# Products of states and w_in for two slices at once, x loads moved, spare matmuls in the prologue

## The chip, the core and the metric

The kernel runs on one core of a Trainium2 chip. The core has a matrix engine (TensorE, "PE" in the profile, with its weight loads as "PEld"), a vector engine (DVE), a scalar engine (ACT), a general engine (POOL) and a queue that issues transfers (SP). Each engine works through its own instructions in program order and waits for the others through semaphores. The metric is the time of one execution on the device in microseconds (us).

## The reference

Inputs are x (8 batches, 8 heads, 512 rows, 64 columns), state (8, 8, 32, 64), w_in (512 x 2048), w_out (2048 x 512) and alpha (2048), all float32. For each batch and head:

```python
scale = 1.0 / np.sqrt(D)
scores = scale * np.matmul(x, state.transpose(0, 1, 3, 2))
a = softmax(scores)                       # over the 32 states
xread = np.matmul(a, state)
a2 = softmax(scale * np.matmul(state, x.transpose(0, 1, 3, 2)))   # over the 512 rows
sread = np.matmul(a2, x)
# heads side by side: tokens of 512 columns, 544 per batch, 4352 in all
h = tokens @ w_in
g = h + np.sin(alpha * h) ** 2 / (alpha + 1e-9)
out = g @ w_out
```

`softmax` stands for the reference's own steps: subtract the largest, take the exponential, divide by the sum.

## The kernel before

**What is computed how.** For the 512 read rows of a batch, `a @ state @ w_in` is regrouped: the product of the states and w_in is taken first. It is called M: 256 rows (8 heads of 32 states, in two groups g of 128) by 2048 columns, per batch. Then `h = a @ M`. The columns of w_in come in four slices of 512 columns; `m_step(b, fs, on_act)` (L354) makes slice fs of M for batch b with eight small matmuls of 64 x 32 weights and 512 columns (L367), into two PSUM banks, one for each g. It then copies both banks to SBUF, by ACT (L376) or DVE (L378), as the table `MA` says.

**The loop.** The main loop runs over nine tiles t of 16 slots f. Tile t < 8 is batch t, and tile 8 holds the state rows of all batches. Slot f makes 128 of the 2048 hidden columns: `mm1` (L381) runs two matmuls (L386) into an `h` bank, ACT takes the sine (L398), POOL (L403) or DVE (L410) squares it, as the table `SQ` says, and `snake` (L413), on DVE, adds the square times 1/alpha to h and writes gT. The snake of a slot is put in two slots later (`LAG = 2`), after the slot's matmuls. `mm2` (L422) multiplies gT of the tile before with w_out; the tables `TWO0`, `TWO1` and `TWO` say how many of its 64 matmuls go into each slot. They fill four output tiles of 128 rows in turn, 16 matmuls each; a full one is copied by ACT (L428) and stored through SP.

**Attention of the next batch.** It is spread over the slots by the table `BATCH`, whose numbers are slots relative to the start of a tile. For the attention steps they are relative to the tile before the batch's own, for W and M to its own tile. L is the load of x (POOL's queue, L143), P the two packs (DVE, L240), T the transpose of x (on PE for batch 1, by a DMA through SP for later ones, L261), S the scores (PE, L277), X their exponential (ACT, L286), R the row sums (DVE, L290), N the division (POOL, or DVE where `ND` says so), A the transpose of the weights (PE or DMA, L267), W the sums over rows (PE, L322, and the column sums Cs, L333), and M the four slices of M. For batch 3 and later one entry serves all.

**Order inside a slot.** The loop emits mm1 and its sine and square, then the PE steps of the table with their copies, then the snake of two slots earlier, then late DVE squares, then mm2, then the other steps ("post": loads, packs, exponentials, sums, transfers). Each engine keeps this order.

**PSUM.** There are eight banks: `psH` has four (the h tiles), `psO` two (outputs of mm2, spare matmuls, W of batch 0), `psX` two (transposes, scores, W, M). M of batch 0, slice 0, lies in psH. A bank is free for its next user when the last reader of the old one is done. `warm_up(n)` issues n matmuls that nothing reads, into a psO bank; `WARM` holds the counts for the prologue.

Of the kernel before, what the change touches and what calls it, by code (L numbers as in the profile page):

```python
# [13 lines left out]
FP32 = mybir.dt.float32  # L14
# [5 lines left out]

BATCH = {0: {'M': (-13, 0, 6, 7), 'MA': ((1, 0), (1, 1), (1, 0), (1, 1))},
 1: {'P': (1, 1),
     'T': (3, 3),
     'S': (3, 3),
     'X': (3, 3),
     'R': (4, 6),
     'N': (7, 10),
     'A': 13,  # L30
     'M': (-5, -2, 3, 9),
     'MA': ((1, 1), (1, 1), (1, 1), (0, 1)),
     'W': (5, 5)},
 2: {'L': -9,
     'P': (-1, -1),
     'T': 1,
     'S': (6, 6),
     'X': (6, 6),
     'R': (7, 9),
     'N': (7, 11),  # L40
     'A': 14,
     'M': (-5, -2, 6, 10),
     'MA': ((1, 1), (0, 0), (1, 1), (0, 1)),
     'W': (-1, -1)},
 3: {'L': -19,
     'P': (-12, -9),
     'T': -9,
     'S': (2, 2),
     'X': (2, 2),
     'R': (4, 5),  # L50
     'N': (4, 11),
     'A': 11,
     'M': (-3, 1, 4, 8),
     'MA': ((1, 1), (1, 1), (1, 1), (1, 1)),
     'W': (-1, -1)}}

SQ = {0: (0, 4, 8, 9, 12, 15),
 1: (3, 5, 6, 7, 11),
 2: (2, 5, 7, 8, 9, 12, 15),
 7: (0, 5, 6, 11, 13, 15),  # L60
 8: (0, 1, 2, 3, 6, 9, 13, 15)}
ND = {1: (), 2: (), 3: (0, 1)}
XS0 = 0

TWO0 = (0, 0, 0, 1, 3, 0, 3, 0, 0, 1, 2, 3, 2, 2, 2, 2)
TWO1 = (2, 5, 3, 1, 1, 3, 3, 0, 3, 4, 9, 3, 0, 1, 4, 1)
TWO = (3, 7, 3, 9, 2, 4, 9, 4, 2, 3, 1, 6, 3, 3, 2, 3)
WARM = (9, 2, 1, 1)
LATER = 6

LOADS = ('i0', 'i1', 'x1', 'o0', 'i2', 'i3', 'o1', 'o2', 'o3')
# [3 lines left out]
def kernel(  # L75
# [21 lines left out]
    FS = 4  # L97
    FW = DFF // FS
# [56 lines left out]
    w_in_sb = wpool.tile([P, Q, DFF], BF16, name="w_in_sb")  # L155
# [24 lines left out]
    stT = const.tile([P, B * G, P], BF16, name="stT")  # L180
# [6 lines left out]
    def warm_up(n):  # L187
        if n:
            wp = psO.tile([P, S], FP32, name="o_ps", tag="o")
        for _ in range(n):  # L190
            nc.tensor.matmul(wp[:], warm[:, 0:P], warm[:], start=True, stop=True)  # L191

    def kind(t):
        return t if t < 2 or t >= B - 1 else 2


    def prep_state():
        st2 = const.tile([P, 16, 2, D], BF16, name="st2")
        for half, copy in ((0, nc.vector.tensor_copy), (1, nc.scalar.copy)):
            js = slice(half * 8, (half + 1) * 8)  # L200
            copy(st2[:, js], st_nat[:, js].unsqueeze(2).to_broadcast([P, 8, 2, D]))
        for half in range(2):
            tp = psH.tile([P, 8, P], BF16, name="st_ps", tag="h")
            for k in range(8):
                nc.tensor.transpose(
                    tp[:, k, :],
                    st2[:, half * 8 + k].rearrange("p r d -> p (r d)"),
                    ident[:],
                )
            for r in range(2):  # L210
                rows = slice(r * D, (r + 1) * D)
                src = tp[rows].rearrange("d k (e r2 jh) -> d e r2 jh k", r2=2, jh=2)
                dst = stT[rows].rearrange(
                    "d bg (h2 r2 jh hf k) -> d (bg h2) r2 jh hf k", h2=2, r2=2, jh=2, hf=2
                )
                nc.scalar.copy(dst[:, :, r, :, half, :], src[:, :, r])

    def prep_alpha():
        tp = psH.tile([P, FT], FP32, name="al_ps", tag="h")
        nc.tensor.transpose(tp[:], alpha_rows[:], ident_f[:])  # L220
        nc.scalar.copy(alpha_sb[:], tp[:])
# [129 lines left out]

    def m_step(b, fs, on_act):  # L354
        if fs == 0:
            Ms[b] = mpool.tile([P, G, DFF], BF16, name="M")
        if b == 0 and fs == 0:
            mp = [psH.tile([P, FW], FP32, name="m0_ps", tag="h") for _ in range(G)]
        else:
            mp = [psX.tile([P, FW], FP32, name="m_ps", tag="px") for _ in range(G)]  # L360
        for h in range(2):
            for g in range(G):
                for r in range(2):
                    rows = slice(r * D, (r + 1) * D)
                    c0 = h * 2 * Ns + r * Ns
                    o0 = h * 2 * Ns + (r ^ g) * Ns
                    nc.tensor.matmul(  # L367
                        mp[g][o0:o0 + Ns, :],
                        stT[rows, b * G + g, c0:c0 + Ns],
                        w_in_sb[rows, 2 * g + h, fs * FW:(fs + 1) * FW],  # L370
                        start=True, stop=True,
                    )
        for g in range(G):
            dst = Ms[b][:, g, fs * FW:(fs + 1) * FW]
            if on_act[g]:
                nc.scalar.copy(dst, mp[g][:])  # L376
            else:
                nc.vector.tensor_copy(dst, mp[g][:])  # L378


    def mm1(t, f):  # L381
# [88 lines left out]
    a.T(1)  # L470
    warm_up(WARM[2])
    a.S(0)
# [6 lines left out]
        load(*w)  # L479
    a.Rs(1)  # L480
    a.N(1, nc.vector)
    m_step(0, 0, (True, True))
    a.W(psO, "o")
    a.Cs()
    warm_up(WARM[3])
    nc.scalar.activation(tiny[:, 1:2], warm[:, 0:1], ACT.Sin)
    a.AT_([0])
    a.AT_([1])
# [5 lines left out]
    pe, post, two = {}, {}, {}  # L494

    def add(d, s, fn, *args):
        d.setdefault(s, []).append((fn, args))
# [8 lines left out]
    for b in range(B):  # L506
        p = BATCH[min(b, 3)]
        s0 = (b - 1) * FT
        if b > 1:
            add(post, s0 + p["L"], load_x, b, 1)  # L510
        if b:
            add(post, s0 + p["P"][0], first, b)
            for g in range(G):
                add(post, s0 + p["P"][g], att, b, "pack", g)
            if b == 1:
                for g in range(G):
                    add(pe, s0 + p["T"][g], att, b, "T", g)
            else:
                add(post, s0 + p["T"], att, b, "T_dma")
            for g in range(G):  # L520
                add(pe, s0 + p["S"][g], att, b, "S", g)
                add(post, s0 + p["X"][g], att, b, "X", g)
                add(post, s0 + p["R"][g], att, b, "Rs", g)
                eng = nc.vector if g in ND[min(b, 3)] else nc.gpsimd
                add(post, s0 + p["N"][g], att, b, "N", g, eng)
            if b == 1:
                add(pe, s0 + p["A"], att, b, "AT_", [0, 1])
            else:
                add(post, s0 + p["A"], att, b, "AT_dma")
        s0 = b * FT  # L530
        if b:
            add(pe, s0 + p["W"][0], att, b, "W")
            add(pe, s0 + p["W"][1], att, b, "Cs")
        add(post, s0 + (p["W"][1] if b else XS0), att, b, "xs")
        for k in range(0 if b else 1, FS):
            add(pe, s0 + p["M"][k], m_step, b, k, p["MA"][k])

    def rows(t, counts, todo):
        for f, c in enumerate(counts):
            two[t * FT + f] = [args for args in todo[:c]]  # L540
            del todo[:c]
# [63 lines left out]
```

The softmax here doesn't subtract the row's maximum and nothing guards it: scores larger than these inputs give would overflow.

## Time and profile before

| what | us |
|---|---|
| median of 5 runs | 232.2 (231.66 to 233.45) |
| the profiled execution | 231.97 |
| its span, first to last instruction | 230.2 |
| PE busy | 214.7 (93%) |
| DVE busy | 174.9 (76%) |
| ACT busy | 169.6 (74%) |
| POOL busy | 106.4 (46%) |
| mean granted PE clock | 0.993 of full |

A row for a group of instructions names line, engine, operation, output and inputs, shapes, count, then busy time and the mean of one in ns, then the idle time before them and what ended it. A row of the timeline has start, duration, engine, line, operation, shapes and count, and in brackets the idle time before it with what ended it. PE's matmuls overlap, so the durations of single ones are longer than the distance between their starts. The page divides the span into 40 slices of 5.75 us; a digit is the busy share in tenths.

### The profile page before, as it was taken

Reading aid. Unit: us, or ns where it says so; the run is one execution under the profiler, and the core shown is the slowest. Engines: PE = TensorE matmul, PEld = TensorE weight load, DVE = VectorE, ACT = ScalarE, POOL = GpSimd, SP = SyncE. Lnnn points to the kernel's source line nnn. Section 1 sums busy time; section 2 is a strip of 40 time slices with the busy share of each in tenths; the row PEclk is TensorE's granted clock in tenths of the full one; section 3 lists DMA queues with packets and bytes.
Section 4 is the critical chain, followed back from the end, with each engine's and each line's share of the span. In section 5 each row is a group of like instructions: output and inputs, shape, how many; then the busy total and the mean of one; then the engine's idle time right before and its main releaser. Section 6 shows DMA issues by size and latency. Waiting matters only on the chain.

```text
span 230.2 us, 4164 instructions
## 1 busy us (share of the span) xinstructions
PE 214.7 (93%) x1508; PEld 103.3 (45%) x1534; DVE 174.9 (76%) x306; ACT 169.6 (74%) x277; POOL 106.4 (46%) x112
## 2 busy tenths in 40 slices
PE   7694799999999999999999999999999999999992
PEld 2443243534444444444444444444444444556562
DVE  3779989989969995989599868987798666754310
ACT  4686987997797679876988698878887876444420
POOL 3855598259652633275236605450543735123300
PEclk9979999999999999999999999999999999999999
DMA  7999999664915381538045802610213111111113
GB/s 218 176 201 207 206 165 126 169 67 120 137 48 137 94 137 46 138 91 140 9 135 134 135 2 102 174 46 4 91 52 87 46 47 46 48 46 47 48 47 93
DMA packets 36662, 23.36 MB, mean 101 GB/s; under 512 B 19728, under 2 KB 32288, under 8 KB 36640
## 3 DMA queue, kind: packets, MB, share of 16 engines
q0 software_dynamic: 11504, 7.87, 24.3%
q1 hardware_dynamic: 24864, 14.95, 22.2%
q8 instruction: 12, 0.20, 0.4%
q10 hardware_dynamic: 272, 0.27, 0.4%
q14 instruction: 10, 0.08, 0.1%
HBM read 17.31 MB, written 8.91 MB: 114 GB/s over the span
## 4 chain that ended last, share of the span: by engine, by line
PE 82%; DVE 6%; DMA 6%; issue 2%; POOL 1%; ACT 1%
PE o_ps L422 48%; PE h_ps L386 21%; DMA xnat<-in_x_dram 5%; PE m_ps L367 4%; PE h_ps L392 3%; DVE gT L413 2%; DMA st_nat<-in_state_dram 2%; PE o_ps L447 2%; PE w_ps L322 1%; PE s_ps L277 1%; DVE xp L240 1%; PE w_ps L333 1%; POOL w_in_sb L166 1%; DVE s L410 1%; ACT L398 0%
## 5 line engine op out<-in xcount | busy, mean ns | idle before, releaser
L403 POOL TENSOR_TENSOR s<-s 128x512 bf16<-128x512 bf16 (+1 forms) x84 | 87.3, 1047 | 103.3 <-ACT s L398 101.4
L422 PE MATMUL o_ps<-w_out_sb,gT 128*128 128x512 bf16 x506 | 132.6, 379 | 2.5 <-issue 1.7
L398 ACT ACTIVATE s<-h_ps,alpha_sb 128x512 bf16<-128x512 f32 (+1 forms) x144 | 94.5, 672 | 36.3 <-PE h_ps L386 23.5
L413 DVE SCALAR_TENSOR_TENSOR gT<-s,inva_sb,h_ps 128x512 bf16<-128x512 bf16 (+1 forms) x144 | 99.6, 709 | 25.1 <-POOL s L403 23.5
L386 PE MATMUL h_ps<-AT,M 128*128 128x512 bf16 x252 | 75.0, 381 | 1.4 <-DVE gT L413 0.8
L422 PEld LDWEIGHTS <-gT 128*128 128x128 bf16 x528 | 48.5, 98 | 56.8 <-issue 6.6
L386 PEld LDWEIGHTS <-M 128*128 128x128 bf16 x256 | 25.0, 98 | 31.1 <-issue 2.8
L376 ACT CAST M<-m_ps 128x512 bf16<-128x512 f32 x59 | 31.8, 594 | 0.9 <-PE m_ps L367 0.9
L410 DVE TENSOR_TENSOR s<-s 128x512 bf16<-128x512 bf16 (+1 forms) x60 | 27.6, 465 | 5.5 <-ACT s L398 5.0
L428 ACT COPY o_sb<-o_ps 128x512 f32<-128x512 f32 x33 | 19.6, 593 | 9.7 <-PE o_ps L422 9.0
L367 PE MATMUL m_ps<-w_in_sb,stT 64*32 64x512 bf16 x256 | 13.3, 393 | 1.9 <-DMA w_in_sb<-in_moe_w_in_dram 1.1
L290 DVE TENSOR_REDUCE R<-E 128x16 f32<-128x512 bf16 x16 | 10.9, 679 | 3.8 <-ACT E L286 3.8
L286 ACT ACTIVATE E<-s_ps 128x512 bf16<-128x512 f32 x16 | 8.9, 595 | 3.0 <-PE s_ps L277 2.8
L367 PEld LDWEIGHTS <-stT 64*32 64x32 bf16 x256 | 3.8, 89 | 15.3 <-issue 15.2
L392 PE MATMUL h_ps<-xs_all,w_in_sb 128*128 128x256 bf16 x64 | 9.6, 273 | 0.0
L342 DVE RECIPROCAL rC<-w_ps 128x128 f32<-128x128 f32 x8 | 7.6, 948 | 2.3 <-PE w_ps L333 2.2
L286 ACT ACT_TABLE_LOAD x7 | 9.0, 1283 | 0.1
L398 ACT ACT_TABLE_LOAD x7 | 9.0, 1283 | 0.1
L240 DVE COPY xp<-xnat 128x1024 bf16<-128x1024 bf16 x14 | 7.6, 554 | 0.9 <-DMA xnat<-in_x_dram 0.9
L392 PEld LDWEIGHTS <-w_in_sb 128*128 128x128 bf16 x64 | 6.3, 98 | 4.1
L277 PE MATMUL s_ps<-stT,xT 128*128 128x64 bf16 x128 | 5.6, 193 | 1.6 <-DVE xT L255 1.3
L191 PE MATMUL o_ps<-warm 128*128 128x512 bf16 x13 | 5.5, 564 | 1.3 <-DVE warm L177 1.3
(52 smaller groups left out, 96.2 us busy)
## 6 DMA issues: line engine op xcount, KB each, us to landing
out_dram<-o_sb SPq DMA_DIRECT2D x32, 256.0 KB, 2.3
xnat<-in_x_dram POOLq DMA_DIRECT2D x7, 512.0 KB, 6.1
w_in_sb<-in_moe_w_in_dram POOLq DMA_DIRECT2D x4, 512.0 KB, 10.8
w_out_sb<-in_moe_w_out_dram POOLq DMA_DIRECT2D x4, 512.0 KB, 16.2
x_first<-in_x_dram SPq DMA_DIRECT2D x2, 512.0 KB, 5.3
st_nat<-in_state_dram SPq DMA_DIRECT2D x1, 512.0 KB, 3.8
out_dram<-o_sb SPq DMA_DIRECT2D x1, 128.0 KB, 2.4
out_dram<-o_sb ACTq DMA_DIRECT2D x1, 128.0 KB, 2.7
```

The costliest lines, as they stand in the source:

```text
L286: nc.scalar.activation(a.E[:, g], a.sp[g][:], ACT.Exp, scale=scale)
L290: nc.vector.reduce_sum(a.R[:, g], E8, axis=AX.X)
L367: nc.tensor.matmul(mp[g][o0:o0 + Ns, :], stT[rows, b * G + g, c0:c0 + Ns], w_in_sb[rows, 2 * g + h, fs * FW:(fs + 1) * FW], start=True, st ...
L376: nc.scalar.copy(dst, mp[g][:])
L386: nc.tensor.matmul(hp[:, :n], Ms[t][:, g, f * P:(f + 1) * P], atts[t].AT[:, g, :], start=(g == 0), stop=(g == G - 1),)
L392: nc.tensor.matmul(hp[:, :n], w_in_sb[:, q, f * P:(f + 1) * P], xs_all[:, q].rearrange("p h k b l -> p (h k b l)"), start=(q == 0), stop=( ...
L398: nc.scalar.activation(s[:, :n], hp[:, :n], ACT.Sin, scale=alpha_sb[:, f:f + 1])
L403: nc.gpsimd.tensor_tensor(s2[:, :n], s[:, :n], s[:, :n], ALU.mult)
L410: nc.vector.tensor_tensor(s2[:, :n], s[:, :n], s[:, :n], ALU.mult)
L413: nc.vector.scalar_tensor_tensor(gT[t][:, f, :n], s2[:, :n], inva_sb[:, f:f + 1], hp[:, :n], ALU.mult, ALU.add)
L422: nc.tensor.matmul(op[:], gT[t][:, ft, st * P:(st + 1) * P], w_out_sb[:, ft, :], start=(ft == 0), stop=(ft == FT - 1),)
L428: nc.scalar.copy(o_sb[:], op[:])
```

## The change

From batch 2 on, `m_step` makes two slices in one call: sixteen small matmuls in a row into four banks (one of psO, one of psH, two of psX), then four copies. The table `SLICES` says so; batches 0 and 1 keep single slices, and batch 0's slice 0 moves from psH to psX. The tables are all rewritten: slots of all steps, which engine copies M, which squares DVE takes, how many mm2 matmuls each slot has. In `BATCH`, the load of x for batch 2 goes from slot 7 to slot 0 of tile 0, and that of later batches from slot 13 to slot 15 of the tile three before their own. The transpose of x goes by one to four slots, that of the weights from slot 11 to 14 for batch 3 and later. Of the two divisions of batch 3 and later one stays on DVE and one goes to POOL. The spare matmuls become 7, 1, 2, 2, 0, 1, 2: two now stand ahead of the first `m_step`, one ahead of batch 1's transposes in slot 3 of tile 0, two ahead of its scores.

```diff
-BATCH = {0: {'M': (-13, 0, 6, 7), 'MA': ((1, 0), (1, 1), (1, 0), (1, 1))},
+BATCH = {0: {'M': (-24, 1, 6, 7), 'MA': ((1, 0), (1, 1), (1, 1), (1, 1))},
  1: {'P': (1, 1),
      'T': (3, 3),
      'S': (3, 3),
      'X': (3, 3),
-     'R': (4, 6),
-     'N': (7, 10),
-     'A': 13,
-     'M': (-5, -2, 3, 9),
-     'MA': ((1, 1), (1, 1), (1, 1), (0, 1)),
+     'R': (3, 7),
+     'N': (11, 9),
+     'A': 14,
+     'M': (-6, 1, 3, 10),
+     'MA': ((1, 1), (1, 1), (1, 1), (1, 1)),
      'W': (5, 5)},
- 2: {'L': -9,
-     'P': (-1, -1),
-     'T': 1,
+ 2: {'L': -16,
+     'P': (1, 3),
+     'T': 5,
      'S': (6, 6),
      'X': (6, 6),
-     'R': (7, 9),
-     'N': (7, 11),
+     'R': (6, 9),
+     'N': (8, 10),
+     'A': 12,
+     'M': (-3, 1, 5, 7),
+     'MA': ((0, 1), (1, 1), (1, 1), (1, 1)),
+     'W': (-1, 0)},
+ 3: {'L': -17,
+     'P': (-13, -11),
+     'T': -8,
+     'S': (0, 2),
+     'X': (2, 2),
+     'R': (5, 8),
+     'N': (9, 12),
      'A': 14,
-     'M': (-5, -2, 6, 10),
-     'MA': ((1, 1), (0, 0), (1, 1), (0, 1)),
-     'W': (-1, -1)},
- 3: {'L': -19,
-     'P': (-12, -9),
-     'T': -9,
-     'S': (2, 2),
-     'X': (2, 2),
-     'R': (4, 5),
-     'N': (4, 11),
-     'A': 11,
-     'M': (-3, 1, 4, 8),
-     'MA': ((1, 1), (1, 1), (1, 1), (1, 1)),
-     'W': (-1, -1)}}
-
-SQ = {0: (0, 4, 8, 9, 12, 15),
- 1: (3, 5, 6, 7, 11),
- 2: (2, 5, 7, 8, 9, 12, 15),
- 7: (0, 5, 6, 11, 13, 15),
- 8: (0, 1, 2, 3, 6, 9, 13, 15)}
-ND = {1: (), 2: (), 3: (0, 1)}
+     'M': (-4, -3, 4, 4),
+     'MA': ((0, 1), (1, 1), (0, 1), (1, 0)),
+     'W': (-2, -2)}}
+
+SQ = {0: (0, 1, 2, 4, 5, 8, 9, 11, 14, 15),
+ 1: (1, 2, 3, 5, 6, 7, 8, 11, 14),
+ 2: (3, 5, 6, 13, 15),
+ 7: (0, 1, 2, 4, 7, 8, 12),
+ 8: (0, 5, 7, 8, 12, 14)}
+ND = {1: (), 2: (), 3: (1,)}
+
+SLICES = {0: ((0,), (1,), (2,), (3,)), 1: ((0,), (1,), (2,), (3,)), 2: ((0, 1), (2, 3)), 3: ((0, 1), (2, 3))}
-TWO0 = (0, 0, 0, 1, 3, 0, 3, 0, 0, 1, 2, 3, 2, 2, 2, 2)
-TWO1 = (2, 5, 3, 1, 1, 3, 3, 0, 3, 4, 9, 3, 0, 1, 4, 1)
-TWO = (3, 7, 3, 9, 2, 4, 9, 4, 2, 3, 1, 6, 3, 3, 2, 3)
-WARM = (9, 2, 1, 1)
+TWO0 = (0, 0, 0, 1, 2, 0, 2, 0, 2, 0, 0, 6, 1, 1, 6, 1)
+TWO1 = (2, 3, 5, 1, 3, 0, 5, 2, 3, 2, 3, 5, 1, 6, 1, 0)
+TWO = (1, 2, 6, 3, 10, 5, 3, 3, 4, 3, 5, 0, 5, 4, 4, 6)
+WARM = (7, 1, 2, 2, 0, 1, 2)
...
-    def m_step(b, fs, on_act):
-        if fs == 0:
+    def m_step(b, slices, on_act):
+        if slices[0] == 0:
             Ms[b] = mpool.tile([P, G, DFF], BF16, name="M")
-        if b == 0 and fs == 0:
-            mp = [psH.tile([P, FW], FP32, name="m0_ps", tag="h") for _ in range(G)]
-        else:
-            mp = [psX.tile([P, FW], FP32, name="m_ps", tag="px") for _ in range(G)]
-        for h in range(2):
+        homes = [(psX, "px"), (psX, "px")]
+        if len(slices) == 2:
+            homes = [(psO, "o"), (psH, "h")] + homes
+        mp = {}
+        for k, (pool, tag) in enumerate(homes):
+            mp[slices[k // G], k % G] = pool.tile([P, FW], FP32, name="m_ps", tag=tag)
+        for fs in slices:
+            for h in range(2):
+                for g in range(G):
+                    for r in range(2):
...
+                        nc.tensor.matmul(
+                            mp[fs, g][o0:o0 + Ns, :],
...
+        for fs in slices:
             for g in range(G):
...
+                dst = Ms[b][:, g, fs * FW:(fs + 1) * FW]
+                if on_act[fs][g]:
+                    nc.scalar.copy(dst, mp[fs, g][:])
+                else:
+                    nc.vector.tensor_copy(dst, mp[fs, g][:])
...
-    m_step(0, 0, (True, True))
+    warm_up(WARM[3])
+    m_step(0, (0,), ((True, True),))
     a.W(psO, "o")
     a.Cs()
-    warm_up(WARM[3])
+    warm_up(WARM[4])
...
             if b == 1:
+                add(pe, s0 + p["T"][0], warm_up, WARM[5])
                 for g in range(G):
                     add(pe, s0 + p["T"][g], att, b, "T", g)
+                add(pe, s0 + p["S"][0], warm_up, WARM[6])
...
-        for k in range(0 if b else 1, FS):
-            add(pe, s0 + p["M"][k], m_step, b, k, p["MA"][k])
+        for slices in SLICES[min(b, 3)][0 if b else 1:]:
+            add(pe, s0 + p["M"][slices[0]], m_step, b, slices, p["MA"])
```

More of the change, by code (lines that the diff above doesn't have):

```diff
@@ L350, in xs @@
                 )
-    def m_step(b, fs, on_act):
-        if fs == 0:
+    def m_step(b, slices, on_act):
+        if slices[0] == 0:
             Ms[b] = mpool.tile([P, G, DFF], BF16, name="M")
-        if b == 0 and fs == 0:
-            mp = [psH.tile([P, FW], FP32, name="m0_ps", tag="h") for _ in range(G)]
-        else:
-            mp = [psX.tile([P, FW], FP32, name="m_ps", tag="px") for _ in range(G)]
-        for h in range(2):
-            for g in range(G):
[L363 to L378, printed above, removed]
+        homes = [(psX, "px"), (psX, "px")]
[8 more added lines that the diff above has]
+                    for r in range(2):
+                        rows = slice(r * D, (r + 1) * D)
+                        c0 = h * 2 * Ns + r * Ns
+                        o0 = h * 2 * Ns + (r ^ g) * Ns
+                        nc.tensor.matmul(
+                            mp[fs, g][o0:o0 + Ns, :],
+                            stT[rows, b * G + g, c0:c0 + Ns],
+                            w_in_sb[rows, 2 * g + h, fs * FW:(fs + 1) * FW],
+                            start=True, stop=True,
+                        )
+        for fs in slices:
+            for g in range(G):
+                dst = Ms[b][:, g, fs * FW:(fs + 1) * FW]
[3 more added lines that the diff above has]
+                    nc.vector.tensor_copy(dst, mp[fs, g][:])
     def mm1(t, f):
```

## The prediction, made before the changed kernel was run

> **What bounds the kernel now.** I read the page's busy times and slices first, then the chain that ended last, then one steady tile instruction by instruction.
>
> ```profile
> PE 214.7 (93%) x1508; PEld 103.3 (45%) x1534; DVE 174.9 (76%) x306; ACT 169.6 (74%) x277; POOL 106.4 (46%) x112
> ...
> PE   7694799999999999999999999999999999999992
> ...
> PEclk9979999999999999999999999999999999999999
> ...
> PE 82%; DVE 6%; DMA 6%; issue 2%; POOL 1%; ACT 1%
> ```
>
> From the sixth slice (about 29 us) PE is never seen idle, and the chain is 82% PE. Before that the chain goes through the landing of x for batch 1. Next, stretches of time (us, PE, PEld, DVE, ACT, POOL busy; clock, DMA share, GB/s):
>
> ```profile
> 17.30:22.50 5.20, 2.13 (x34) 1.53 (x34) 4.78 (x6) 3.18 (x6) 3.39 (x3) 1.00 1.24 206
> 22.50:36.00 13.50, 11.96 (x84) 5.04 (x85) 12.20 (x23) 12.42 (x21) 10.21 (x11) 1.00 1.14 174
> 36.00:57.00 21.00, 20.22 (x168) 9.32 (x170) 19.93 (x37) 18.04 (x29) 12.95 (x13) 1.00 0.71 127
> 105.00:129.00 24.00, 23.63 (x167) 10.81 (x169) 20.33 (x35) 20.00 (x34) 11.04 (x10) 1.00 0.45 101
> ```
>
> Tiles 0 and 1 (to 57 us) load DVE to 90 and 95%; a steady tile (105:129) is set by PE alone. The Sin of slot 0 starts every 23.89 us from tile to tile. A busy PE need not be at peak, so I price starts, not spans. A step of states times w_in (L367) on PE:
>
> ```profile
> 123.90 0.59 PE L386 MATMUL h_ps<-AT,M 128*128 128x512 bf16 x2
> 124.43 0.41 PE L367 MATMUL m_ps<-w_in_sb,stT 64*32 64x512 bf16 x8
> 124.77 0.82 PE L422 MATMUL o_ps<-w_out_sb,gT 128*128 128x512 bf16 x3
> 125.43 0.59 PE L386 MATMUL h_ps<-AT,M 128*128 128x512 bf16 x2
> ```
>
> Three L422 take 0.66 us, so a 512-column matmul costs 0.216. The two before the step end their issue at 124.33; the next begins at 124.77. The step costs 0.44 us, 0.216 of it streaming (eight small tiles stream together), 0.22 getting in and out of the small tiles. A steady tile sums to 96 x 0.216 + 4 x 0.435 + S 0.465 + W 0.56 + Cs 0.36 = 23.87: PE waits for nothing there.
>
> **Part 1, two slices in one step (batches 2 to 7).** Twelve pairs replace 24 steps. If the second eight matmuls follow the first without a drain, a pair costs 0.435 + 0.216 = 0.651 instead of 0.87: 12 x 0.219 = **-2.63 us**. The trace shows no two such rounds in a row. Ends: the second round costs 0.216, or a whole 0.435 and nothing is saved. The Trainium skill, "TensorEngine Tiling (Array Packing)", Restrictions, says that column tiling disables fast weight load, which speaks for an exposed load: one load of 0.09 us (L367 PEld mean 89 ns) before each second round would leave 12 x 0.13 = -1.5. I take -2.63: the page's Cs row, also column-tiled, issues eight matmuls with loads of 109 ns in 0.36, so those loads hide.
>
> **What the pair's four banks cost.** A pool gives out the buffer that was freed first in program order. A pair takes one psO, one psH and both psX. The psH buffer is the critical one: the snake of slot f-2 is queued after the pair, so the next mm1 gets the very bank that the pair used, and must wait for its copy. In tiles 3 to 6 the pair (2,3) is at slot 4, just behind Exp of slot 2:
>
> ```profile
> 107.87 0.59 PE L386 MATMUL h_ps<-AT,M 128*128 128x512 bf16 x2
> ```
>
> ```profile
> 108.56 0.69 ACT L398 ACTIVATE s<-h_ps,alpha_sb 128x512 bf16<-128x512 f32 x1 [0.74 <-PE h_ps L386]
> 109.27 1.28 ACT L286 ACT_TABLE_LOAD   x1
> 110.56 1.08 ACT L286 ACTIVATE E<-s_ps 128x512 bf16<-128x512 f32 x2
> 111.66 1.28 ACT L398 ACT_TABLE_LOAD   x1
> 112.96 0.69 ACT L398 ACTIVATE s<-h_ps,alpha_sb 128x512 bf16<-128x512 f32 x1
> ```
>
> Call the start of mm1 of slot 2 zero (107.87). ACT: Sin 2 at 0.69, table and two Exp and table, Sin 3 at 5.09, Sin 4 at 5.67 (ACT starts 0.58 apart), then the pair's first ACT copy 6.25 to 6.85; PE may go on at 6.9. PE by the new table: slot 2 mm1 0.43 + half of S 0.23 + 6 mm2 1.30 = 1.96; slot 3 0.43 + 3 x 0.216 = 1.08; slot 4 0.43 + pair 0.65 + 10 x 0.216 = 3.24; so mm1 of slot 5 is due at 6.28 and waits **0.63**. Four tiles: **+2.5 us**. Everything behind that mm1 on PE waits too. Ends: nothing, if Exp is earlier than here, or 0.9 if ACT carries other copies. Before, mm1 of slot 5 took a bank freed by a snake, and only the two psX banks hung on ACT.
>
> In the same pair psX is free at 3.8 (end of Exp) against a need at 3.78: nothing. The psO bank's copy is given to DVE, 4.0 to 4.7, needed at 5.0: hidden, with 0.3 to spare. The pair (0,1) at slot 12: zero at its mm1, Sin 12 at 0.69, ACT copy 1.28 to 1.87, mm1 of slot 13 due at 0.43 + 0.65 + 5 x 0.216 = 2.16: hidden; snake 9 (for the bank) and the DVE copy (for op 3) have 0.15 us or less to spare, cost 0 to 0.3 each, taken as 0. Pair of tile 7: no Exp there, hidden.
>
> Tile 2 is different: its pair is at slot 5 and takes the psO bank of the output tile that ended in slot 4. That tile's copy follows Sin 4 on ACT, 6.25 to 6.85; the pair is due at 0.43 + 0.23 + 1.30 + 1.08 + 0.43 + 2.16 + 0.43 + 0.09 = 6.15 and waits 0.75. The x load of batch 4 now is issued after slot 15 of tile 1 instead of 13, and its pack is at slot 3 instead of 4; landing takes 6.1 us, which puts the pack at about 5.6 and snake 2, whose bank the pair also needs, at 7.0: **+0.85** in all. In later tiles the same load lands near 3.1, before DVE is needed at 4.0.
>
> The Trainium skill, "TensorEngine Tiling (Array Packing)", PSUM Bottleneck, warns that tiling speeds up TensorE but not the copies out of PSUM. The totals say it doesn't matter: ACT is busy 20.0 of 24, and five copies instead of eight go to it (-3 x 0.6), three to DVE. By the totals the sum stays -2.63; by the rule, placed at the slot, 3.35 of waits eat it. I take the slot.
>
> **Part 2, prologue and tiles 0 and 1.** PE waits for batch 1's x, which no edit moves (same load order):
>
> ```profile
> 17.69 2.33 DVE L240 COPY xp<-xnat 128x1024 bf16<-128x1024 bf16 x2 [0.86 <-DMA xnat<-in_x_dram]
> 20.05 0.75 DVE L413 SCALAR_TENSOR_TENSOR gT<-s,inva_sb,h_ps 128x512 bf16<-128x512 bf16 x1
> 20.71 1.28 DVE L255 COPY xT<-x_ps 128x1024 bf16<-128x1024 bf16 x2
> ```
>
> ```profile
> 17.52 3.39 POOL L403 TENSOR_TENSOR s<-s 128x512 bf16<-128x512 bf16 x3 [2.87 <-ACT s L398]
> ```
>
> Two packs take 2.33 beside POOL's squares; the median of all packs is 0.42. Squares 1 and 2 move to DVE, so the packs should take some 1.2 (-1.1), and a square of 0.46 gets ahead of xT: **-0.6**. Spare matmuls (13 become 15) sit where PE waits for w_in (1.1 us), pack (1.6 and 0.6) and xT (0.8): free, 0.22 each. They hide only there; uncovered, three in tile 0 cost 0.65. The halved clock from 12.8 to 16.2 (third digit, 7) may vanish; PE then waits for the pack all the same, so nothing. Other work on DVE up to the end of tile 1: seven squares more (7 x 0.46 = +3.2), three M copies fewer (3 x 0.69 = -2.1), the packs' -1.1: about nothing, on an engine that is full there, so I leave it out of the sum and in the range.
>
> A new wait: the transpose of batch 2's x.
>
> ```profile
> 37.37 3.12 SPq L261 DMA_TRANSPOSE xT<-xp  x1
> ```
>
> ```profile
> 43.89 0.40 PE L277 MATMUL s_ps<-stT,xT 128*128 128x64 bf16 x8
> ```
>
> It started at 37.4 beside batch 3's load and landed 5.1 later, 1.4 before use. Now its second pack is in slot 3 of tile 1 and it stands behind it, at about 41.8; at the median 3.7 it lands at 45.5, while S is due near 44.1 to 44.5. PE would wait 0 to 1.5, I take **+0.8**, as PE has some slack to DVE there. AT's transpose (median 2.7) goes from slot 11 to 14 on SP's queue, behind the store of output tile 2: it lands some 7.0 after mm1 of slot 12, needed at 7.7; hidden, at +1.5 if a store holds SP. The x loads take 0.94 us of POOL each as before, in other places.
>
> **Tail.** Tile 8 has two squares fewer on DVE; PE has 4 L422 between slots to cover them: 0.
>
> **Sum** against the profiled execution, 231.97 us with span 230.2 (1.8 outside it): -2.63 + 2.5 + 0.85 - 0.6 + 0.8 = +0.9, 232.9. The median of the runs shown is 232.2, 0.2 above the profiled one; that is less than my terms are sure to, and I leave 232.9.
>
> **Rivals.** (A) *The waits are covered*: faster. For it: PE has no wait in a steady tile today, 10 mm2 stand behind the pair, ACT has 4 us spare per tile. Against it: the ACT rows above. 231.97 - 2.63 = 229.3, with prologue +0.2 and small waits, **229.8**. (B) forecast: saving eaten, **232.9**. (C) *The late transpose and DVE decide tiles 1 and 2*: slower. S waits the full 1.5, and DVE, idle 3 us for batch 4's x, passes another 1 us to PE in tile 2: **234.6**. It decides once xT lands later than 44.5. (D) *No saving*: the second round pays its own drain, so the change doesn't do what it says: waits stay, **235.5**.
>
> **How the numbers follow.** Chances: A 0.30, B 0.37, C 0.23, D 0.10. Half a per cent (1.16 us, about what can be told apart here) puts A under 231.04, B within, C and D above 233.36: faster 0.30, same 0.37, slower 0.33. Leaving out 0.1 at each end: 229.5 to 235.2. B's own range is 231.2 to 233.3.
>
> **What would show it.** L367 x16 with next start 0.65 after the mm1: part 1 right; 0.87: D. ACT releasing an mm1 at slot 5 of tiles 3 to 6 by about 0.6: B; none: A. A wait of PE s_ps for the transpose near 45: C's start. Packs at 17.7 near 0.6 each: part 2. The forecast is wrong if banks are given out in another order, or if the tile length falls to 23.45.

## The result, and the profile after

The changed kernel took **231.63 us** (median of 43 runs, 230.9 to 234.33), the kernel before in the same sessions 232.54 (80 runs). The ratio is **0.9973**, with a 95% interval of 0.9959 to 0.9987. Here and below a ratio leaves out runs more than 1.5% above the fastest of the same kernel, while a median keeps them, so the two can differ by up to 0.6 us. The change is a small gain of 0.27%, inside the half per cent that I had called the limit of what can be told, and on the other side of 1 than my 232.9. The profiled execution took 231.18 (before 231.97), its span is 229.4 (before 230.2).

From the page of the changed kernel: busy time, two rows of the slices, and the chain that ended last.

```profile
PE 211.3 (92%) x1508; PEld 102.3 (45%) x1536; DVE 170.8 (74%) x309; ACT 164.5 (72%) x266; POOL 111.5 (49%) x120
...
PE   5777899799989999998999999999997999999993
...
PEclk9999999999999999999999999999999999999999
...
PE 73%; DMA 12%; ACT 7%; issue 3%; DVE 2%; POOL 1%; SPq 0%; ACTq 0%
```

PE has lost 3.4 us of busy time and the span only 0.8. The chain says where to look: it was 82% PE and 6% DMA, now it is 73% and 12%. After the tenth slice PE has an 8 near 65 and 105 us and a 7 near 175, where before it had nines throughout. Two of the stretches of time, in the columns of the prediction:

```profile
17.30:22.50 5.20, 3.82 (x41) 2.23 (x42) 4.93 (x10) 4.54 (x6) 1.04 (x1) 1.00 1.23 202
105.00:129.00 24.00, 23.63 (x173) 11.12 (x173) 19.11 (x35) 19.02 (x30) 13.56 (x13) 1.00 0.45 99
```

PE does 3.82 us of work in the first stretch instead of 2.13: the transposes and scores of batch 1 come sooner. The second, a steady tile, is as full as before. Whom PE waited for, over the whole execution (total us, times, longest); L393 is mm1, L279 the scores, L373 the step of states times w_in:

```profile
...
PE h_ps L393 <- DMA AT<-A: 1.9, 2, 1.3
...
PE s_ps L279 <- DMA xT<-xp: 1.5, 1, 1.5
...
PE m_ps L373 <- ACT o_sb L435: 0.6, 1, 0.6
```

Two waits were in the prediction: the late transpose of batch 2's x, and the copy of an output tile ahead of tile 2's pair. The row of AT, two waits for the transpose of the weights, was not.

The ledger is made of tile lengths: from the first sine of a tile to the first sine of the next (for tile 8, to its last), in us, in one profiled execution of each kernel. "in order", "shift", "early x" and "early AT" are experiments 1, 2, 3 and 9 below.

| tile | before | after | in order | shift | early x | early AT |
|---|---|---|---|---|---|---|
| 0 | 21.36 | 19.79 | 19.28 | 20.04 | 19.69 | 20.07 |
| 1 | 21.20 | 21.61 | 21.61 | 21.61 | 21.35 | 21.61 |
| 2 | 23.44 | 24.52 | 24.46 | 26.72 | 24.51 | 24.51 |
| 3 | 23.88 | 24.27 | 24.93 | 23.47 | 24.16 | 23.47 |
| 4 | 23.89 | 23.47 | 24.02 | 23.47 | 23.47 | 23.47 |
| 5 | 23.89 | 23.47 | 24.02 | 24.75 | 23.47 | 23.47 |
| 6 | 23.89 | 24.93 | 25.42 | 23.47 | 25.20 | 23.47 |
| 7 | 22.07 | 21.37 | 21.37 | 21.37 | 21.37 | 21.37 |
| 8 | 19.50 | 19.52 | 19.52 | 19.51 | 19.52 | 19.52 |

Tile 1 starts 1.95 earlier (34.61 instead of 36.56). Tiles 4 and 5 take 23.47; I had named 23.45 as a sign against my forecast. Tiles 3 and 6, which the same table of slots rules, are 0.80 and 1.46 longer than tiles 4 and 5, and differ from each other: nothing in the order of the work explains that.

**The pair.** The timeline of tile 4 (start, duration, engine, line, operation) with the pair of slot 4, on PE:

```profile
109.10 0.59 PE L393 MATMUL h_ps<-AT,M 128*128 128x512 bf16 x2
109.62 0.67 PE L373 MATMUL m_ps<-w_in_sb,stT 64*32 64x512 bf16 x16
110.45 2.11 PE L429 MATMUL o_ps<-w_out_sb,gT 128*128 128x512 bf16 x9 [0.16 <-issue]
112.39 0.59 PE L393 MATMUL h_ps<-AT,M 128*128 128x512 bf16 x2
```

and on ACT:

```profile
111.15 1.27 ACT L405 ACTIVATE s<-h_ps,alpha_sb 128x512 bf16<-128x512 f32 x2
112.30 1.07 ACT L383 CAST M<-m_ps 128x512 bf16<-128x512 f32 x2
```

Sixteen small matmuls now take the place of two groups of eight. (Slot 4 has ten L429; the trace lacks the record of one, which is the 0.16 of "issue".) From the mm1 of slot 4 to that of slot 5 it is 3.29; less 0.43 for mm1 and 2.16 for the ten, 0.70 is left for this pair. mm1 of slot 5 starts at 112.39. The pair's first ACT copy runs from 112.30 to about 112.9. My forecast had this mm1 wait for that copy; it starts before the copy is done, at 6.33 after mm1 of slot 2 (106.06) where I had it due at 6.28.

**The transposes of the weights.** Two windows of the DMA view of the changed kernel, each 40 slices long, with busy share in tenths and GB/s. First 100.0 to 104.3, in tile 3:

```profile
DMA  0000999999609999990000000000008999943963
GB/s 0 0 0 0 362 362 400 495 343 305 172 3 291 245 286 269 214 45 0 0 0 0 0 0 10 17 10 12 10 10 167 288 295 281 166 52 48 76 24 19
...
q8 instruction: 1, 0.02, 1.9%
...
AT<-A SPq DMA_TRANSPOSE x1, 4.2
```

then 124.3 to 127.1, in tile 4:

```profile
DMA  0000027899999898104999999999999820000000
GB/s 0 0 0 0 0 117 293 351 468 380 439 439 439 263 293 234 30 8 113 230 282 289 293 293 293 282 293 285 293 289 282 173 48 4 0 0 0 0 0 0
...
AT<-A SPq DMA_TRANSPOSE x1, 2.7
```

In both, a store runs first (the block to about slice 16 in the second, 11 in the first) and then the transpose at nearly 300 GB/s. In tile 4 it runs in one go. In tile 3 it stops after six slices; for some 1.3 us first nothing and then 10 to 17 GB/s moves, and then it goes on. One packet of the instruction queue, 16 KB, is under way from 101.31 to 102.64, and SP's queue starts its next packet at 102.64. There are 12 such packets in an execution with 3,044 matmuls and weight loads, one for every 254 of them: it is PE's code being fetched.

### The profile page after: what moved, and what is told of

Same layout as the page of the kernel before. It is cut to its first block, busy times and chain, and to the rows that moved or that the text cites. A ratio compares the mean times of both kernels' runs of the same rounds, so it can differ in the third digit from the quotient of the medians.

```text
span 229.4 us, 4186 instructions
## 1 busy us (share of the span) xinstructions
PE 211.3 (92%) x1508; PEld 102.3 (45%) x1536; DVE 170.8 (74%) x309; ACT 164.5 (72%) x266; POOL 111.5 (49%) x120
## 4 chain that ended last, share of the span: by engine, by line
PE 73%; DMA 12%; ACT 7%; issue 3%; DVE 2%; POOL 1%; SPq 0%; ACTq 0%
PE o_ps L429 42%; PE h_ps L393 20%; DMA xnat<-in_x_dram 4%; DMA AT<-A 4%; PE h_ps L399 3%; PE m_ps L373 3%; ACT s L405 3%; ACT M L383 2%; DMA xT<-xp 2%; DMA st_nat<-in_state_dram 2%; PE s_ps L279 2%; PE o_ps L454 2%; PE w_ps L324 1%; ACT o_sb L435 1%; POOL w_in_sb L168 1%
## 5 line engine op out<-in xcount | busy, mean ns | idle before, releaser
L429 PE MATMUL o_ps<-w_out_sb,gT 128*128 128x512 bf16 x510 | 131.6, 379 | 2.2 <-issue 1.9
L420 DVE SCALAR_TENSOR_TENSOR gT<-s,inva_sb,h_ps 128x512 bf16<-128x512 bf16 (+1 forms) x144 | 99.6, 708 | 23.5 <-POOL s L410 22.2
L393 PE MATMUL h_ps<-AT,M 128*128 128x512 bf16 x247 | 73.1, 379 | 2.8 <-DMA AT<-A 1.9
L429 PEld LDWEIGHTS <-gT 128*128 128x128 bf16 x528 | 49.5, 98 | 57.3 <-issue 5.1
L393 PEld LDWEIGHTS <-M 128*128 128x128 bf16 x256 | 24.5, 98 | 32.4 <-DMA AT<-A 2.9
L417 DVE TENSOR_TENSOR s<-s 128x512 bf16<-128x512 bf16 (+1 forms) x57 | 24.6, 437 | 5.3 <-ACT s L405 4.4
L383 ACT CAST M<-m_ps 128x512 bf16<-128x512 f32 x48 | 25.4, 601 | 0.5 <-PE m_ps L373 0.5
L385 DVE CAST M<-m_ps 128x512 bf16<-128x512 f32 x16 | 10.6, 689 | 9.1 <-PE m_ps L373 9.1
L373 PE MATMUL m_ps<-w_in_sb,stT 64*32 64x512 bf16 x256 | 11.4, 383 | 1.2 <-ACT o_sb L435 0.6
L300 POOL TENSOR_TENSOR A<-E,rR 128x512 bf16<-128x512 bf16 x8 | 8.4, 1048 | 5.2 <-DVE rR L293 5.2
L242 DVE COPY xp<-xnat 128x1024 bf16<-128x1024 bf16 x14 | 5.5, 407 | 3.9 <-DMA xnat<-in_x_dram 3.9
L279 PE MATMUL s_ps<-stT,xT 128*128 128x64 bf16 x128 | 6.2, 193 | 2.3 <-DMA xT<-xp 1.5
L373 PEld LDWEIGHTS <-stT 64*32 64x32 bf16 x256 | 3.2, 89 | 10.7 <-issue 8.6
```

The lines of the kernel that those rows point to most:

```text
L373: nc.tensor.matmul(mp[fs, g][o0:o0 + Ns, :], stT[rows, b * G + g, c0:c0 + Ns], w_in_sb[rows, 2 * g + h, fs * FW:(fs + 1) * FW], start=True ...
L383: nc.scalar.copy(dst, mp[fs, g][:])
L393: nc.tensor.matmul(hp[:, :n], Ms[t][:, g, f * P:(f + 1) * P], atts[t].AT[:, g, :], start=(g == 0), stop=(g == G - 1),)
L417: nc.vector.tensor_tensor(s2[:, :n], s[:, :n], s[:, :n], ALU.mult)
L420: nc.vector.scalar_tensor_tensor(gT[t][:, f, :n], s2[:, :n], inva_sb[:, f:f + 1], hp[:, :n], ALU.mult, ALU.add)
L429: nc.tensor.matmul(op[:], gT[t][:, ft, st * P:(st + 1) * P], w_out_sb[:, ft, :], start=(ft == 0), stop=(ft == FT - 1),)
```

## The experiments

Each kernel was measured against the kernel before on its own chip, in three groups: 1 to 4 (before 232.51 us), 5 to 8 (232.56) and 9 to 11 (232.86).

**1. Banks in order.** My +2.5 us rested on the pair's psH bank going to the next mm1. This edit gives out the four psH banks in the order in which the program frees them.

```diff
+    h_free = [0, 1, 2, 3]
...
-            homes = [(psO, "o"), (psH, "h")] + homes
+            hk, tag = h_tag()
+            homes = [(psO, "o"), (psH, tag)] + homes
...
+        if len(slices) == 2:
+            h_free.append(hk)
...
+        h_free.append(hk)
```

> The changed kernel with the four h banks given out strictly in the order in which the program frees them, as the prediction took it; nothing else moves. In the changed kernel the mm1 after the pair at slot 4 took the bank of the snake of slot 2, not the pair's own, and did not wait. Theory (the wait was worked out rightly, only the bank was wrong): PE waits 0.5 to 0.7 us for the pair's ACT copy before mm1 of slot 5 in tiles 3 to 6, total 2.0 to 2.8 us over the changed kernel, so about 233.8. Rival (ACT is early enough anyway, the bank does not matter): within 0.4 us of the changed kernel's 231.6.

Measured: 233.38 us, ratio 1.0063 (1.0036 to 1.0090), against 0.9973 for the change as it was made: 0.9% or 2.1 us more. From its list of PE's waits (L406 is mm1, L393 the copies of M):

```profile
PE h_ps L406 <- ACT M L393: 1.5, 4, 0.4
```

Four waits, one in each of tiles 3 to 6, and tiles 4 and 5 longer by 0.55. The wait that I had worked out as 0.63 exists and costs 0.55 as soon as the bank goes where I said it goes (0.4 of it shows as idle time of PE). In the changed kernel it doesn't: in the built program, at slot 4 of tile 4, the pair has bank 2 and the next mm1 bank 0, which the snake of slot 2 had freed. At slot 12 the next mm1 does get the pair's own bank, but there the copy is done in time, as I had forecast. The mechanism and its size were right; the rule by which the pool gives out banks did not hold at the one slot where it mattered.

**2. The code moved.** If the code fetch holds the transpose, 36 short matmuls that nothing reads, all before tile 1's scores, move every later fetch to another place in the tiles.

```diff
+    def shift(n):
+        wp = psO.tile([P, S], FP32, name="o_ps", tag="o")
+        for _ in range(n):
+            nc.tensor.matmul(wp[:, 0:D], warm[:, 0:P], warm[:, 0:D], start=True, stop=True)
...
+    shift(20)
     prep_state()
...
                 add(pe, s0 + p["T"][0], warm_up, WARM[5])
+                add(pe, s0 + p["T"][0], shift, 16)
```

> The changed kernel with 36 more spare matmuls of 64 columns (20 after the first spare ones, 16 ahead of batch 1's transposes), all where PE waits; they move every later PE instruction 72 places back. In the changed kernel the weights' transpose took 4.2 and 4.8 us in tiles 3 and 6 instead of 2.7, and in both a 16 KB instruction fetch fell into it; PE waited 0.6 and 1.2 us. Theory (the fetch holds the transpose): fetches come some 70 instructions earlier in the work, outside all six transposes, all six take 2.7 to 2.9, PE's wait for them goes, -1.4 to -1.9 us, about 229.9. Rival (the store issued 0.5 us ahead, or the place of the transpose in the tile, holds it): tiles 3 and 6 stay slow, 231.5 to 232.

Measured: 232.73 us, ratio 1.0017 (0.9994 to 1.0041). The expected gain was missed: tiles 3 and 6 went down to 23.47, and tiles 2 and 5 went up to 26.72 and 24.75. Their transposes now took 4.93 and 4.65, those of tiles 3 and 6 only 2.74 and 2.73. The DMA view of this kernel from 77.1 to 82.2, in tile 2, shows the same gap in a transpose that had been whole:

```profile
DMA  0008999980699990500000000000000799999999
...
q8 instruction: 1, 0.02, 1.3%
...
AT<-A SPq DMA_TRANSPOSE x1, 4.9
```

Only the count of PE's instructions ahead was changed, and the long transposes moved with the fetches. As a cure it is useless: with transposes every 23.5 us and a fetch every 14 to 22, this shift only picks another victim.

**3. Batch 2's x earlier.** The second pack leaves slot 3 of tile 1 and the transpose follows it.

```diff
-     'P': (1, 3),
-     'T': 5,
+     'P': (0, 1),
+     'T': 1,
```

> The changed kernel with batch 2's packs in slots 0 and 1 of tile 1 (instead of 1 and 3) and its transpose behind slot 1 (instead of 5). Theory (the late transpose costs PE 1.5 us in tile 1, which nothing else then needs): transpose starts near 37, beside the load of batch 3, lands near 42.2, PE waits 0.3 or less, -1.0 to -1.3 us, about 230.5. Rival (DVE is full in tile 1, PE's wait is only time that DVE needs): -0.4 or less, 231.2 or more.

Measured: 230.97 us, ratio 0.9955 (0.9931 to 0.9980). PE's wait of 1.5 for the transpose is gone, and in its place stands one for VectorE (DVE):

```profile
PE s_ps L279 <- DVE xs_all L347: 1.1, 1, 1.1
```

Of 1.5 us, 0.7 came out of the time by the medians (0.4 by the ratios) and 0.26 out of tile 1 in the profile. What PE had waited for was only in part the transpose; VectorE was nearly as late.

**4. Squares 1 and 2 of tile 0 back on GpSimd (POOL).** The packs of batch 1 took 2.33 before, beside three squares on GpSimd.

```diff
-SQ = {0: (0, 1, 2, 4, 5, 8, 9, 11, 14, 15),
+SQ = {0: (0, 4, 5, 8, 9, 11, 14, 15),
```

> The changed kernel with the squares of slots 1 and 2 of tile 0 given back to POOL. Theory (two packs beside POOL's squares take 1.2 us each instead of 0.43, and tile 0's gain of 1.9 us is mostly that): the packs take 2.0 to 2.4 us in all, the scores of batch 1 come 1.2 to 1.7 later, total +1.0 to +1.7, about 233. Rival (tile 0 gained by the matmul clock kept up and by fewer M copies): within 0.4 us of the changed kernel, 231.6.

Measured: 231.73 us, ratio 0.9993 (0.9967 to 1.0019), whose interval overlaps that of the change. In the profile the packs took 2.23 again and tile 0 took 22.16, but PE's clock was halved for some microseconds from 19.0 in that execution, so its tile length can't be read as the price of the packs. The contention is there; its price in the time is 0.1 us by the medians and 0.5 by the ratios, below the expected 1.0 to 1.7, and the interval doesn't exclude nothing. Experiment 11 asks the same from the other side.

**5. The spare matmuls alone, on the kernel before.**

```diff
-WARM = (9, 2, 1, 1)
+WARM = (7, 1, 2, 2, 0, 1, 2)
...
+    warm_up(WARM[3])
     m_step(0, 0, (True, True))
...
-    warm_up(WARM[3])
+    warm_up(WARM[4])
...
+                add(pe, s0 + p["T"][0], warm_up, WARM[5])
...
+                add(pe, s0 + p["S"][0], warm_up, WARM[6])
```

> The kernel before with the changed kernel's spare matmuls alone (7, 1, 2, 2, 0, 1, 2 instead of 9, 2, 1, 1, with two ahead of the first m_step, one ahead of batch 1's transposes, two ahead of its scores). In the runs so far the kernel before spends 3 to 12 us at half clock in nearly every run, 5 in the middle, the changed one nothing in most. Theory (the spares keep the clock, and that is worth about 0.25 us for each us at half clock): most runs without half clock after the start, -0.9 to -1.5 us against before, about 231.2. Rival (they only fill PE's waits, as the prediction took it, and the half clock lies where PE waits anyway): within 0.4 us of before.

Measured: 232.46 us, ratio 0.9978 (0.9942 to 1.0014): the interval holds both a gain and none. Inconclusive by itself. In the profiled execution tile 0 took 20.41, 0.95 less than before, and tile 1 took 23.37, 2.17 more: PE waited 2.1 there for VectorE, whose packs of batch 2 took 0.87 and 1.26 beside GpSimd's squares.

**6. The old counts of spares in the changed kernel.**

```diff
-WARM = (7, 1, 2, 2, 0, 1, 2)
+WARM = (9, 2, 1, 0, 1, 0, 0)
```

> The changed kernel with the spare matmuls of before (9, 2, 1, one after Cs, none ahead of m_step, transposes and scores). Theory (spares keep the clock): most runs spend 3 to 7 us at half clock again and the median rises by 0.9 to 2.0 us to 232.5 to 233.6, so that the rest of the change is no gain at all. Rival (they are only fill): within 0.4 us of the changed kernel's 231.6.

Measured: 232.00 us, ratio 0.9976 (0.9955 to 0.9997), beside 0.9973 with the new counts. The expected rise to 232.5 or more did not come. The spares do what a reader would guess: the mean granted clock, times the span, tells how long PE ran at half clock, and it was at most 1.7 us in 36 of 44 runs with the new counts and in 6 of 22 with the old. But it hardly pays. The six runs of the old counts without such a stretch have a median of 231.14, the eight with the next longer one 232.01; the changed kernel without it has 231.6. These few runs suggest that a spared stretch is worth some 0.9 us and that the added spares cost some 0.5 of it back; they don't show it. Together the spares are worth 0 to 0.4 us by ratios and medians, and my "nothing" was near enough.

**7. No pairs.** All slices of M one by one again, everything else as changed.

```diff
-     'M': (-3, 1, 5, 7),
+     'M': (-3, -2, 5, 8),
...
-     'M': (-4, -3, 4, 4),
+     'M': (-4, -1, 4, 8),
...
-SLICES = {0: ((0,), (1,), (2,), (3,)), 1: ((0,), (1,), (2,), (3,)), 2: ((0, 1), (2, 3)), 3: ((0, 1), (2, 3))}
+SLICES = {0: ((0,), (1,), (2,), (3,)), 1: ((0,), (1,), (2,), (3,)), 2: ((0,), (1,), (2,), (3,)), 3: ((0,), (1,), (2,), (3,))}
```

> The changed kernel with single slices again, each into the two psX banks, slices 1 and 3 in slots 15 and 8 (batch 2: 14 and 8), all other tables as changed. Theory (a pair saves 0.22 us of PE, 12 of them, and costs 0.65 us in tile 2 alone): steady tiles 23.9 instead of 23.47, +2.0 to +2.8 us with the same waits for transposes, about 234. Rival (the pair's gain is lost in waits for its copies): +0.5 or less.

Measured: 236.02 us, ratio 1.0147 (1.0113 to 1.0181), 4.0 us over the change by the ratios. That is more than the pairs can save: a steady tile took 24.68, 1.21 over 23.47, and two pairs account for 0.44. The other 0.77 is, by the starts, time lost around the single steps at the slots that I chose (two of them, at 111.92 and 129.10, take 0.26 and 0.55 more than 0.435); the last of them in tile 4 breaks off after two matmuls:

```profile
129.10 0.39 PE L373 MATMUL m_ps<-w_in_sb,stT 64*32 64x512 bf16 x2
129.65 0.40 PE L373 MATMUL m_ps<-w_in_sb,stT 64*32 64x512 bf16 x6 [0.15 <-DVE xs_all L347]
129.99 1.47 PE L429 MATMUL o_ps<-w_out_sb,gT 128*128 128x512 bf16 x6
```

The run shows that the pairs matter, not how much; that is read from tiles 4 and 5, below.

**8. A smaller shift together with the early x.** Experiment 3 with 14 and 13 short matmuls at the places of experiment 2.

```diff
+    shift(14)
     prep_state()
...
+                add(pe, s0 + p["T"][0], shift, 13)
...
-     'P': (1, 3),
-     'T': 5,
+     'P': (0, 1),
+     'T': 1,
```

> The changed kernel with batch 2's packs and transpose early (packs in slots 0 and 1, transpose behind slot 1), and 27 short spare matmuls (14 and 13) instead of the 36 that moved the instruction fetches from the transposes of tiles 3 and 6 into those of tiles 2 and 5. Reckoned from the two placements seen, fetches now start from 1.5 us before to 0.2 before the transposes of tiles 3 and 6 and some 3 us after those of tiles 2 and 5. Theory (a fetch that starts within some 2.5 us after the issue of a transpose holds it): all six weights' transposes take 2.7 to 2.9, PE has no wait for them, tiles 3 to 6 all 23.47, 1.3 to 2.0 below the early variant's 230.97, about 229.3. Rival (some transpose is slow whatever the placement): 230.5 or more.

Measured: 230.04 us, ratio 0.9916 (0.9881 to 0.9951), between the theory and the rival. Tiles 3 to 6 took 23.47 to 23.53; the fetch at 80.4 fell 2.5 us after the issue of tile 2's transpose, which took 4.82, and tile 2 took 26.03. Tile 1 took 22.80, 1.45 more than in experiment 3, with 1.8 of PE waiting for VectorE, which the theory did not have; why, this run doesn't show. The profiled execution, 231.76, was the slowest of the eight.

**9. The transpose of the weights earlier.** The fetches stay; the transpose goes. In batches 3 to 7 it goes back from slot 14 to 11, where it was before the change, and with it the division that it waits for.

```diff
-     'N': (9, 12),
-     'A': 14,
+     'N': (9, 11),
+     'A': 11,
```

> One edit to the changed kernel, for batches 3 to 7: the second normalisation of A goes from slot 12 to slot 11 and the transpose of A from slot 14 to slot 11, which puts it ahead of the third store of the output tile on SP's queue. Theory (an instruction fetch of PE that starts while the transpose is under way holds it): AT is issued 1.0 to 1.5 us earlier, at 98.6 to 99.1 in tile 3 and 169.9 to 170.3 in tile 6, so it is done before the fetches near 101.3 and 173.4 begin and takes 2.7 instead of 4.2 and 4.8. PE's waits of 0.58 and 1.24 for AT go, tiles 3 and 6 take 23.5 to 23.8, and the time is 1.5 to 1.9 us below the changed kernel's: about 229.9, ratio to before 0.989 to 0.991. Rival (the long transposes do not set the time of the runs without a profile, or the store behind them and the earlier work on DVE take as much): ratio 0.995 to 0.999.

Measured: **228.96 us**, ratio **0.9862** (0.9822 to 0.9903). Tiles 3 and 6 fell to 23.47, 0.80 and 1.46 less. The queue of SP in tile 3, first of the kernel before:

```profile
99.03 0.34 SPq L434 DMA_DIRECT2D out_dram<-o_sb  x1
99.61 1.24 SPq L267 DMA_TRANSPOSE AT<-A  x1
```

then of the changed kernel:

```profile
99.60 0.33 SPq L441 DMA_DIRECT2D out_dram<-o_sb  x1
100.10 1.27 SPq L269 DMA_TRANSPOSE AT<-A  x1
```

and of this one:

```profile
97.06 1.23 SPq L269 DMA_TRANSPOSE AT<-A  x1
99.43 0.33 SPq L441 DMA_DIRECT2D out_dram<-o_sb  x1
```

The transpose is now issued 3.0 us earlier (I had expected 1.0 to 1.5), so it is over before the fetch at 101.1, and it goes ahead of the store instead of behind it. (The store is not what held it: in the kernel before, too, one is issued 0.58 ahead of the transpose, which then took 2.73.) In this kernel too one transpose meets a fetch, in tile 4 at 120.5, and takes 3.38 instead of 2.7; there are 3 us to spare by then, and tile 4 has its 23.47. By the ratios the time fell by 2.6 us, which their intervals leave open between 1.6 and 3.6: near the 2.26 of the two tiles, and no proof of more than the 1.5 to 1.9 that I had expected from PE's waits as listed.

**10. Both.** Experiments 3 and 9 together.

```diff
-     'P': (1, 3),
-     'T': 5,
+     'P': (0, 1),
+     'T': 1,
...
-     'N': (9, 12),
-     'A': 14,
+     'N': (9, 11),
+     'A': 11,
```

> The same edit together with the early transpose of batch 2's x (batch 2's packs at slots 0 and 1, its transpose at slot 1 of tile 1). Theory: both gains add, since they lie in different tiles: 230.97 less 1.5 to 1.9 is 229.1 to 229.5, ratio to before 0.985 to 0.988; tiles 3 to 6 each take 23.5. Rival: no more than the early x alone, ratio 0.994 to 0.997.

Measured: **228.55 us**, ratio 0.9852 (0.9793 to 0.9910), the fastest of all. Tiles 3 to 6 are at 23.47 and tile 1 at 21.35. The early x adds about as much to this as it did alone, but the interval is too wide to tell it from nothing.

**11. The two squares on VectorE, on the kernel before.**

```diff
-SQ = {0: (0, 4, 8, 9, 12, 15),
+SQ = {0: (0, 1, 2, 4, 8, 9, 12, 15),
```

> The kernel before with one edit: squares 1 and 2 of tile 0 on VectorE instead of GpSimd, as the change has it. Theory (GpSimd's squares slow the packs of batch 1, and the packs set when tile 1 can begin): the two packs near 17.7 take about 0.43 each instead of 2.33, the first sine of tile 1 comes at 35.0 to 35.6 instead of 36.56, and the time falls by 1.0 to 1.5 us, ratio 0.9935 to 0.996. My prediction put the packs at 1.2 and the gain at 0.6. Rival (the packs become short but what follows them waits for something else by then, or they are long only in some executions): ratio 0.998 to 1.001.

Measured: 232.03 us, ratio 0.9969 (0.9943 to 0.9996). VectorE's timeline of this kernel:

```profile
19.28 0.42 DVE L410 TENSOR_TENSOR s<-s 128x512 bf16<-128x512 bf16 x1 [0.53 <-ACT s L398]
19.62 0.76 DVE L240 COPY xp<-xnat 128x1024 bf16<-128x1024 bf16 x2
```

The two packs take 0.76 together instead of 2.33. Tile 0 took 19.91 instead of 21.36. The first sine of tile 1 did not come early, since w_in was late in this execution and tile 0 began at 17.01. The gain in the time is 0.1 to 1.3 us, 0.7 in the middle: below what theory expected, and where the prediction had it. The profiled executions say more: in the ten kernels with these squares on VectorE tile 0 took 19.09 to 20.07, in the three with them on GpSimd 20.41 to 22.16: before 21.36, experiment 4 22.16, and experiment 5, where only one of the two packs was slow, 20.41. But before and experiment 4 also ran at half clock for a while.

## Why the prediction was wrong

**Part 1 (-2.63): right.** The pair costs 0.65 (0.70 at slot 4): the second eight start 0.226 after the first, so there is no drain between them, and no exposed weight load either: one of 0.09 would have made it 0.31 and left -1.5. Tiles 4 and 5, with two pairs each and no disturbance, are shorter by 0.42, twice 0.21 where I had 0.219. Tile 7 goes from three single steps to one pair, which makes 0.65, and is shorter by 0.70.

**The wait of mm1 of slot 5 (+2.5): the step that failed first.** "A pool gives out the buffer that was freed first in program order. ... so the next mm1 gets the very bank that the pair used." The next mm1 got a bank that a snake had freed, and does not wait. Experiment 1 forces the order that I assumed and gets 0.55 for each of tiles 4 and 5, and 2.1 us in the time. So this term was not mis-sized; it belonged to another program. I noted in advance that the forecast is wrong "if banks are given out in another order", and did not look for the order itself.

**The transpose of the weights (0): the step that failed second, the other way.** "It lands some 7.0 after mm1 of slot 12, needed at 7.7; hidden." This is right to a tenth where nothing disturbs: in tile 4 it landed at 127.11, 7.0 after that mm1. But 0.7 us is all that the change left it, by moving it from slot 11 to 14. Before, it was issued in time to have 2 us to spare. In tiles 3 and 6 the fetch of PE's code made it take 4.16 and 4.79 us where the median is 2.73, and 0.80 and 1.46 came through to the tiles. I had given a price to a store that holds SP, "+1.5", but not to anything that holds the transfer itself. Experiments 2 and 9 show the cause: the slow transposes move with the fetches, and go when the transpose is moved away. Its price is 2.26 us in the profile and 2.6 (1.6 to 3.6) in the time.

Across the profiled executions of all thirteen kernels there are 78 transposes of the weights. In 17 of them a fetch began between 0.6 us before and 2.5 us after the issue; these took 3.33 to 5.15 us. The 61 others took 2.70 to 2.81. No transpose is on the wrong side. The trace of before held an example that I overlooked, in a transpose of x. That of batch 3, issued at 48.12, took 5.1 us where those of batches 4 to 7 took 3.6 to 3.7; its DMA view from 47 to 54 has the gap and the fetch:

```profile
DMA  0000000000000599999999000000089969799300
...
q8 instruction: 1, 0.02, 1.0%
...
xT<-xp SPq DMA_TRANSPOSE x1, 5.1
```

In all thirteen kernels the transpose of batch 3's x took 4.16 to 5.34 us in the five that a fetch met in this way, and 3.62 to 3.64 in the eight others. Of these 22 held transposes 18 show a pause of 0.4 to 1.5 us on SP's queue, and it ends each time within 0.02 us of the end of the fetch's packet; in the four others the fetch began within 0.6 us of the issue.

The Trainium skill, "Runtime: NRT & Kernel Launch", Instruction fetch mechanics, says that code is refilled in blocks of 16 KiB, 256 instructions, at a cost that is "mostly hidden". The count fits, 12 packets of 16 KB here. Hidden it is for PE, which shows no wait at a fetch in these traces (beyond the 0.16 that a missing record leaves); it is not for a transpose that is under way.

**Tile 2's pair (+0.85): right, a little large.** PE waited 0.655 for ACT's copy of the output tile, the only wait of a pair for a copy out of PSUM. Tile 2 is longer by 1.08 in all; another 0.41 of it is the column sums of batch 2, which the change moved into it out of tile 1; its two pairs cost 1.30, as much as the three single steps that it had before (3 x 0.435).

**Batch 2's x (+0.8 out of 0 to 1.5): right in kind, at the upper end.** The transpose was issued at 39.30 and landed at 43.41; PE waited 1.5. Tile 1 is longer by only 0.41, largely because the column sums left it, one pair replaced two single steps (0.22 less) and small waits of PE there (0.9 us before, 0.2 besides this one after) went. By experiment 3 the time gets 0.4 to 0.7 back when it is moved, so 0.8 was a little large for the time.

**Packs (-0.6) and spares (0).** The packs fell to 0.76 for both, lower than my 1.2, and tile 1 began 1.95 us earlier in the profile, where I had 0.6. How much of that is the packs' is not settled: the time gives 0.1 to 1.3 (experiment 11) and nothing to 0.5 (experiment 4), the lengths of tile 0 in the profiles 1 us or more. The rest of it, a fuller clock and fewer small waits of PE in tile 0 (4.8 us in total before, 3.0 after), I can't divide further. In the sum of the profile this term was mis-sized by about 1.3 us: the third step that failed, its cause in part open.

**The sum.** By the profile: tile 1 starts at -1.95, tile 1 itself +0.41, tiles 2 to 7 +0.97, the rest -0.23, together -0.80. I had +0.9. The bank term was 2.5 too high, the held transposes 2.26 too low, and these two nearly cancel; most of what is left is the prologue, and it decides the sign: with the -0.6 that I had for it the sum would be +0.55. That 231.63 lay no further from my forecast is luck. Of my rivals A, "the waits are covered", names the right mechanism for the pairs, and experiment 9, which is the change without the held transposes, shows where it leads: 228.96, a little below A's 229.8.

## What to carry to other kernels

When an edit moves a transfer later, write down the slack that is left after it, and ask what else can lengthen the transfer: here 0.7 us was enough in the tiles that a code fetch missed and not enough in the two that it hit. Where a gain shows in some tiles of a uniform loop and not in others, look for something with a period of its own, and compare the tiles one by one before looking for a cause in the order of the work. Which buffer a pool hands out is a fact to be read from the built program, not a rule to be assumed, when a forecast hangs on it.

## What the runs showed of the hardware that I had not expected

- A DMA transpose from SBUF to SBUF that takes 2.7 us is stopped by a fetch of PE's code, and takes 3.3 to 5.2 us. The fetch is one packet of 16 KB, under way for 1.3 us in tile 3 of the changed kernel; the transpose goes on when the packet ends. Why the transpose has to wait the runs don't show.
- Adding instructions to PE in the first 20 us can slow a tile 40 us and more later (experiment 2: tile 2 from 24.52 to 26.72), because it moves the places at which code is fetched.
- A copy of 128 x 1024 two-byte elements on VectorE takes 0.42 us alone, and 1.05 to 1.26 in the packs of batch 1 that started 0.16 to 0.28 us after one of GpSimd's multiplications had (before, experiments 4 and 5). One that started 0.07 us ahead of such a multiplication took 0.43 (experiment 5). This shows only in part in the time (experiments 4 and 11).
